# A new instruction order for a gated mix of windowed attention and a token-mixing MLP, with the last result tile cut at three quarters of its columns

## The chip, the core and the metric

The kernel runs on one core of a Trainium2 chip. The metric is the device time of one execution in microseconds (us). A core has five engines that run side by side, each with its own queue of instructions: TensorE (PE; its weight loads are listed as PEld), VectorE (DVE), ScalarE (ACT), GpSimd (POOL) and SyncE (SP), which here only starts DMA transfers. Instructions of one engine stay in order; engines wait for each other through semaphores.

## What is computed

```python
def reference(A_x, A_wqkv, A_wo, B_x, B_w1, B_b1, B_w2, B_b2, gate_w):
    # x: 1 x 2048 x 512, bf16
    def _A_ref(x, wqkv, wo):                      # 32 heads of 16, causal window of 256 keys
        qkv = (x @ wqkv) ...                      # q, k, v
        scores = einsum("bhqd,bhkd->bhqk", q, k) * 16 ** -0.5
        mask = (0 <= i - j < 256)
        p = softmax(where(mask, scores, -1e9))
        return einsum("bhqk,bhkd->bhqd", p, v) ... @ wo
    def _B_ref(x, w1, b1, w2, b2):
        h = layernorm(x, axis=-1)
        u = gelu(einsum("bsd,sf->bdf", h, w1) + b1)     # S = 2048 -> F = 1376
        y = einsum("bdf,fs->bds", u, w2) + b2           # back to 2048
        return y.transpose(0, 2, 1)
    g = sigmoid((x * gate_w).sum(-1, keepdims=True))
    return g * _A_ref(x, ...) + (1 - g) * _B_ref(x, ...)
```

## The kernel before

The 2048 tokens are 16 tiles of 128. The work is cut into about 1,100 tasks, and each task issues a few instructions on one engine. The names of tasks are used all through this document:

- `x`, `xt`, `wqk`, `wv`, `gw`, `w1_`, `w2_`, `wo`: loads, on SP. `xt1` to `xt3` are transposing DMAs of 512 tokens each (L464); `gw` copies the 512 weights of the gate to all 128 partitions (L510). `vs` and `vz` copy rows of V between partitions (L720 to L731).
- `warm` fills PE before data is there (L593). `xta` transposes the first 512 tokens on PE (L610), and `xtc` copies the result out of PSUM.
- `q`, `k`, `v` are projections (L672). `q2_1.0` is the first pair of matmuls of row block 2 of q for the tokens 512 to 1023. `qc`, `kc`, `vc` copy them out of PSUM. The projections of the first 512 tokens start with two half-width matmuls, since the token columns arrive in halves.
- `s5.v1`, `s5.C`: score matmuls of query tile 5 (L923 for the full key tiles, L1024 for the corners of the window, L979 for the last tile). `e` are their exponentials on ACT (L875), `m` the masks, on POOL (L539) or DVE (L888, L955). `pv5.2`: the products with V (L1069). `n1` to `n4` normalise a tile on DVE and put it back transposed (L1160 to L1195).
- `bs`, `ba`, `pow`, `h`: layer norm on DVE and POOL. `gl`, `gatem`, `gatee`, `ez`: the gate's dot products (L803), exponentials and their spreading.
- `u`: the first MLP product (L672, and L1240 for the last 96 columns), `ub` its bias (L439, L441), `gelu` one block of four ACT instructions (L1272).
- `y`: the second MLP product of a result tile, 11 matmuls with `w2` and four with `wo` into the same PSUM bank; `f` scales it (ACT L439, DVE L442), `o` writes it to memory (L1324).

A task such as `u`, `y` or a later `q`, `k`, `v` is flexible. It runs as 128-column weights, or as four 32-column pieces side by side when its neighbours have that shape already, because a change of the shape costs PE time. The set `THEN` says after which attention task the pieces are used.

The order on each engine is not found by a scheduler at build time. `PLAN` writes it out, one string of task names for each engine, and the digits after a name are its buffers: `s1.v0:26` means that the scores go to the pairs of PSUM banks that start at 2 and at 6, `e1.v0.0:1` that the exponential goes to buffer 1. PSUM has eight banks (0 to 7). A task that takes a bank waits until the engine that used it last is done with it:

```python
if who not in (None, t.engine):
    tc.add_manual_dep(first, ins.name, ..., reason="psum bank")
```

`arrange` walks the five strings and merges them into one emission order, with cost numbers that stand in the tasks (`2.3`, `0.58` and so on). These numbers change no instruction. They decide how the engines' instructions are interleaved in the program, and for a POOL task whether it is given a wait for the DVE instruction before it[...].

Of the kernel before, what the change touches and what calls it, by code (L numbers as in the profile page):

```python
# [84 lines left out]
def arrange(tasks):  # L85
# [21 lines left out]
    while len(order) < len(tasks):  # L107
# [83 lines left out]
        warm:3 xta0.0.1:7 xta0.0.0:4 warmb xta0.1.1:5 xta0.1.0:6 q3_0.0:4 q2_0.0:1 q0_0.0:7 q3_0.1 q0_0.1 q1_0.0:3  # L191
        k3_0.0:5 k0_0.0:6 q1_0.1 k1_0.0:2 k1_0.1 q1_0.2 q0_0.2 q1_0.3 k3_0.1 k0_0.1 q0_0.3 q0_0.4 k1_0.2 k0_0.2
        k0_0.3 q1_0.4 k1_0.3 k2_0.0:0 k0_0.4 q2_0.1 k3_0.2 k1_0.4 q2_0.2 k2_0.1 k3_0.3 k3_0.4 q2_0.3 s0.v0:62
        q3_0.2 q2_0.4 k2_0.2 k2_0.3 v0.0:5 q3_0.3 k2_0.4 v0.2 s1.v0:62 q3_0.4 v2.0:0 v2.2 v3.0:5 v3.2 q0_1.0:4
        s0.v1:60 q0_1.2 q3_1.0:2 q3_1.2 v5.0:3 v5.2 s0.C:06 k2_1.0:4 k3_1.0:5 k2_1.2 s-1.C:60 k3_1.2 q1_1.0:3
        q1_1.2 s1.v2:60 v1.0:2 v1.2 v10.0:5 pv-1.0:6 v13.0:3 k3_2.0:4 v10.2 v13.2 s1.C:60 v15.0:2 v15.2 biast:5
        k2_2.0:3 k3_2.2 k2_2.2 v12.0:2 v12.2 s1.v1:04 pv0.0:6 v14.0:3 pv0.1 pv0.2 v14.2 k1_1.0:2 s1.v3:40 k1_1.2
        v7.0:3 v7.2 s2.v2:60 v6.0:2 v6.2 v4.0:4 k0_1.0:5 k0_1.2 s2.v3:26 v4.2 pv1.0:0 pv1.1 pv1.2 pv1.3 pv1.4
        v8.0:5 v8.2 s2.v0:62 q2_1.0:4 k1_2.0:5 k1_2.2 v9.0:7 v9.2 q2_1.2 s3.v1:20 k0_2.0:6 v11.0:7 k0_2.2 v11.2
        u2.0:5 s2.v1:02 u2.2 u3.0:4 u2.4 s2.C:62 u3.2 u3.4 u3.6 u3.8 s3.v0:06 u3.10 u3.12 u3.14 u2.6 s3.v3:62  # L200
        pv2.0:0 u2.8 pv2.1 pv2.2 pv2.3 u7.0:4 s3.v2:26 u7.2 u2.10 u7.4 s3.C:20 u7.6 u7.8 u7.10 s4.C:26 u2.12 u7.12
        u2.14 u7.14 s5.v0:02 pv3.0:6 pv3.1 pv3.2 q0_2.0:5 pv3.3 q0_2.2 s4.v2:20 u10.0:4 u10.2 u10.4 u10.6 s4.v0:26
        u10.8 u10.10 u10.12 u6.0:5 s4.v1:20 u10.14 u6.2 u6.4 s4.v3:06 u6.6 q3_2.0:3 u6.8 q3_2.2 u6.10 s5.v2:60
        u0.0:4 u0.2 u0.4 s5.v3:62 u0.6 pv4.0:0 pv4.1 u6.12 u0.8 pv4.2 pv4.3 s5.v1:26 u6.14 u0.10 u0.12 s5.C:02
        u0.14 q2_2.0:5 q2_2.2 s6.v3:06 k3_3.0:4 k3_3.2 q1_2.0:3 q1_2.2 u5.0:2 s6.v1:46 u5.2 u5.4 u1.0:3 u1.2
        s6.v2:04 pv5.0:6 pv5.1 u1.4 u1.6 pv5.2 pv5.3 u5.6 s6.v0:04 u1.8 u1.10 u1.12 s6.C:46 u5.8 u5.10 u1.14
        s8.v1:04 u5.12 u5.14 pv6.0:6 pv6.1 pv6.2 pv6.3 s7.v2:40 k1_3.0:2 k1_3.2 u4.0:3 s7.v0:06 u4.2 u4.4 u9.0:2
        s7.C:04 u4.6 u4.8 u4.10 s8.v0:64 u4.12 u9.2 u4.14 u9.4 s7.v1:04 u9.6 q0_3.0:3 q0_3.2 s8.C:60 u9.8 u9.10
        u9.12 s7.v3:64 u8.0:3 u9.14 u8.2 u8.4 s10.v0:06 u8.6 u8.8 u8.10 u8.12 pv7.0:4 s8.v2:60 pv7.1 u8.14 pv7.2
        pv7.3 q2_3.0:2 s8.v3:60 k0_3.0:3 k0_3.2 q3_3.0:5 q3_3.2 q2_3.2 pv8.0:0 pv8.1 pv8.2 pv8.3 k2_3.0:6 q1_3.0:3  # L210
        k2_3.2 q1_3.2 y0.0:2 y7.0:7 s9.v2:04 y4.0:6 y0.2 y0.4 y0.6 y0.8 y7.2 y0.10 y0.11 y0.13 y4.2 y4.4 y4.6
        s9.v3:20 y4.8 y4.10 y4.11 y4.13 s9.C:24 y7.4 y7.6 y2.0:6 s10.v3:04 y7.8 y2.2 y2.4 y7.10 s11.v2:24 y7.11
        y2.6 y7.13 y2.8 s9.v0:40 y2.10 y2.11 y8.0:7 y8.2 s9.v1:42 y2.13 y8.4 y8.6 s10.v1:04 y8.8 y1.0:6 y8.10 y8.11
        s10.v2:02 y8.13 pv9.0:4 pv9.1 y1.2 pv9.2 pv9.3 s10.C:02 y9.0:7 y9.2 y9.4 s12.v2:40 y9.6 y1.4 y9.8 y1.6
        s12.C:24 y9.10 y1.8 y9.11 y1.10 y9.13 s11.v0:02 y1.11 pv10.0:4 y1.13 pv10.1 pv10.2 pv10.3 s11.v1:20 y5.0:7
        y5.2 y10.0:6 s11.C:24 y10.2 y10.4 y10.6 s11.v3:04 y5.4 y5.6 y5.8 y5.10 s12.v0:02 y5.11 y5.13 y10.8 y10.10
        s12.v3:42 y10.11 pv11.0:0 y10.13 pv11.1 pv11.2 pv11.3 s12.v1:24 y3.0:7 y3.2 y3.4 s13.v0:40 y11.0:6 y3.6
        y3.8 y3.10 s13.v1:24 y3.11 y3.13 y11.2 s13.C:20 y11.4 y11.6 y11.8 y11.10 s13.v3:40 y11.11 y11.13 pv12.0:2
        pv12.1 pv12.2 pv12.3 s14.v1:40 y6.0:6 y6.2 y12.0:7 s13.v2:20 y6.4 y6.6 y6.8 y6.10 s14.v0:24 y12.2 y6.11
        y6.13 s14.C:02 y12.4 y12.6 pv13.0:4 pv13.1 pv13.2 pv13.3 s14.v2:02 y12.8 y12.10 y13.0:6 y12.11 s15.C:04  # L220
        y12.13 y13.2 s14.v3:20 y13.4 y14.0:7 y13.6 y13.8 y13.10 s15.A:40 pv14.0:2 pv14.1 pv14.2 pv14.3 y14.2 y13.11
        s15.B:04 y14.4 y15r.0:3 y14.6 y14.8 y15l.0:2 y15r.2 y14.10 pv15.0:0 pv15.1 pv15.2 y15r.4 y15r.6 y15r.8
        y14.11 y15l.2 y13.13 y15l.4 y15r.10 y14.13 y15l.6 y15l.8 y15r.11 y15r.13 y15l.10 y15l.11 y15l.13
    """,
    ACT="""
        xtc0.0.0 xtc0.0.1 kc0_0 kc1_0 kc3_0 e0.v0.1:a e0.v0.0:6 kc2_0 vc0 e1.v0.0:8 vc2 e1.v0.1:b e0.v1.0:9
        e0.v1.1:7 vc3 e0.C.0:4 e0.C.1:5 vc5 e-1.C.1:3 e-1.C.0:2 kc3_1 gatee0 e1.v2.0:0 kc2_1 vc1 e1.v2.1:2 vc10
        vc13 e1.C.1:3 vc15 e1.C.0:1 kc3_2 kc2_2 vc12 e1.v1.0:a e1.v1.1:9 vc14 e1.v3.1:6 kc1_1 e1.v3.0:7 e2.v2.0:c
        vc7 e2.v2.1:d kc0_1 e2.v3.1:8 e2.v3.0:6 vc8 e2.v0.0:b e2.v0.1:a kc1_2 vc9 e3.v1.1:e e3.v1.0:f kc0_2
        e2.v1.1:9 e2.v1.0:7 e2.C.0:3 e2.C.1:2 e3.v0.1:4 e3.v0.0:5 ub3 e3.v3.1:b e3.v3.0:a e3.v2.0:c e3.v2.1:d  # L230
        e3.C.0:9 e3.C.1:8 e4.C.0:3 e4.C.1:2 ub7 e5.v0.1:4 e5.v0.0:5 e4.v2.0:9 e4.v2.1:e e4.v0.0:f e4.v0.1:d
        e4.v1.1:c e4.v1.0:8 e4.v3.0:7 e4.v3.1:6 e5.v2.0:1 e5.v2.1:0 e5.v3.1:f e5.v3.0:d e5.v1.0:e e5.v1.1:c
        e5.C.0:8 e5.C.1:9 e6.v3.1:7 gatee1 e6.v3.0:6 gatee2 e6.v1.0:h e6.v1.1:g e6.v2.0:4 e6.v2.1:5 gatee3
        e6.v0.1:f e6.v0.0:e e6.C.0:d e6.C.1:c e8.v1.1:1 e8.v1.0:0 ub1 e7.v2.1:h e7.v2.0:g e7.v0.0:7 e7.v0.1:6
        e7.C.1:a e7.C.0:b e8.v0.1:d e8.v0.0:c e7.v1.0:f e7.v1.1:e e8.C.0:3 e8.C.1:2 e7.v3.0:5 e7.v3.1:4 e10.v0.1:9
        e10.v0.0:8 e8.v2.0:7 e8.v2.1:e e8.v3.1:f e8.v3.0:6 gelu e9.v2.0:i e9.v2.1:e e9.v3.0:j e9.v3.1:c e9.C.1:g
        e9.C.0:2 e10.v3.1:f e10.v3.0:3 e11.v2.1:b e11.v2.0:a e9.v0.0:d e9.v0.1:h e9.v1.0:7 e9.v1.1:6 e10.v1.0:0
        e10.v1.1:1 e10.v2.0:5 e10.v2.1:d e10.C.0:h e10.C.1:g e12.v2.0:j e12.v2.1:i e12.C.0:4 e12.C.1:e e11.v0.0:c
        e11.v0.1:2 f1:2 e11.v1.0:d e11.v1.1:f e11.C.1:9 e11.C.0:5 e11.v3.0:h e11.v3.1:g e12.v0.1:8 e12.v0.0:3
        e12.v3.0:7 e12.v3.1:c f10:0 e12.v1.1:f e12.v1.0:d e13.v0.0:9 e13.v0.1:6 e13.v1.0:a e13.v1.1:b e13.C.1:2  # L240
        e13.C.0:g e13.v3.1:h e13.v3.0:5 e14.v1.1:e e14.v1.0:4 e13.v2.0:i e13.v2.1:j e14.v0.0:f e14.v0.1:c e14.C.0:8
        e14.C.1:d e14.v2.0:9 e14.v2.1:5 e15.C.0:3 e15.C.1:7 e14.v3.1:2 e14.v3.0:i e15.A.0:j e15.A.1:0 e15.B.0:i
        e15.B.1:h f13:1 f14:2 f15r:3
    """,
    DVE="""
        zeros parity const bs3:0 bs1:1 xtc0.1.0 xtc0.1.1 ba1 bs0:1 ba3 ba0 bs2:0 ba2 qc0_0 qc1_0 bs6:0 bs5:1 qc2_0
        h0 qc3_0 gl0 gl1 h1 gl3 qc0_1 h2 gl2 gl5 h3 gatem0 qc3_1 ba5 qc1_1 bs7:1 ba6 ba7 n1-1:c bs8:1 ez0 bs4:0
        biasc ba4 ba8 bs9:0 n2-1 bs11:1 nz-1:1 ba9 n3-1:0 m1.C.1 n10:4 bs13:0 n20 ba11 ba13 bs10:1 bs12:0 ba10 vc6
        ba12 bs15:1 bs14:0 ba15 nz0:1 ba14 h9 h11 vc4 n11:0 h12 h10 h15 h5 h14 h8 h7 h6 h13 h4 qc2_1 vc11 m2.v0.1
        m2.v2.0 n30:1 gl7 m2.C.0 m2.v1.0 m2.v1.1 n21 m2.C.1 gl8 gl6 gl13 gl12 m3.v1.1 n12:6 m3.v0.1 gl4 gl11 nz1:1  # L250
# [39 lines left out]
def kernel(  # L290
# [205 lines left out]
    def small_loads():  # L496
# [8 lines left out]
            ),  # L505
            nc.sync.dma_start(biases[N1:NB, :], B_b2[:].rearrange("(t p) -> t p", p=P)),
        ]

    dgw = load(
        "gw", lambda: nc.sync.dma_start(gwr[:], bass.AP(tensor=gate_w.tensor, offset=gate_w.offset, ap=[[0, P], [1, D]])),  # L510
        1.2, 2.3,
    )

    def set_constants():
        nc.vector.memset(eps[:], EPS)
# [876 lines left out]
```

## Time and profile before

The median of 7 runs was 201.0 us (200.54 to 201.48). The profile is of one execution.

| | before |
|---|---|
| profiled execution | 200.54 us |
| its span, first to last instruction | 198.8 us |
| around the span | 1.74 us |
| PE busy | 188.1 us (95%), 4140 matmuls recorded |
| ACT busy | 171.3 us (86%) |
| DVE busy | 153.5 us (77%) |
| POOL busy | 83.6 us (42%) |
| granted TensorE clock | 1.000 |

Consecutive instructions of one engine overlap a little, so busy times are sums of durations and not of occupied time. For PE, the distance between the starts of neighbouring matmuls is the better measure, and the text uses it. Some 33 of the 4173 matmuls have no record in the trace; each leaves what looks like a gap of one matmul.

### The profile page before, as it was taken

How to read it: one execution, taken by the hardware profiler on the slowest of the kernel's cores; microseconds unless marked ns; L12 is line 12 of the kernel's file. 1: busy time of each engine (PE TensorE's matmuls, PEld its weight loads, DVE VectorE, ACT ScalarE, POOL GpSimd, SP SyncE). 2: the span in 40 equal slices, each digit the busy share in tenths (PEclk: the TensorE clock that was granted, in tenths of full speed). 3: DMA queues.
4: the chain of work that ended last, by engine and by line, in shares of the span. 5: the costliest groups of instructions: out<-in, count | busy, mean ns of one | idle time of the engine just before them, and what ended most of it. 6: DMA issues, size and time to landing. Idle time of an engine off the chain costs nothing.

```text
span 198.8 us, 9301 instructions
## 1 busy us (share of the span) xinstructions
PE 188.1 (95%) x4140; PEld 93.7 (47%) x4173; DVE 153.5 (77%) x323; ACT 171.3 (86%) x200; POOL 83.6 (42%) x122
## 2 busy tenths in 40 slices
PE   6999989999998999999999999999999999999993
PEld 3643344434445635454544554433636354545572
DVE  2889977998898997897879689538388847595871
ACT  2299989999989887979999799799899999898743
POOL 8911499933024551651170940055553100566410
PEclk9999999999999999999999999999999999999999
DMA  5999789993010100101299740003111011112002
GB/s 146 357 174 210 188 252 278 360 319 80 3 32 3 35 0 13 22 5 32 40 389 407 290 157 2 31 30 91 50 33 56 3 57 31 44 32 62 30 3 79
DMA packets 23187, 22.02 MB, mean 111 GB/s; under 512 B 7564, under 2 KB 21260, under 8 KB 23148
## 3 DMA queue, kind: packets, MB, share of 16 engines
q1 hardware_dynamic: 23148, 21.44, 36.5%
q8 instruction: 32, 0.52, 1.2%
q14 instruction: 7, 0.06, 0.1%
HBM read 15.60 MB, written 2.10 MB: 89 GB/s over the span
## 4 chain that ended last, share of the span: by engine, by line
PE 81%; POOL 7%; ACT 6%; issue 3%; DVE 2%; POOLq 0%; DVEq 0%; ACTq 0%
PE pb L672 58%; PE ps L1069 9%; PE ps L923 9%; POOL et L539 4%; ACT et L875 4%; PE ps L1024 3%; PE pb L1240 2%; POOL VA L577 1%; ACT XT L875 1%; POOL XT L539 1%; ACT XT L604 1%; ACT KT L604 1%; PE pb L610 1%; ACT VA L604 0%; DVE ug L441 0%
## 5 line engine op out<-in xcount | busy, mean ns | idle before, releaser
L875 ACT ACTIVATE et<-ps 128x1024 bf16<-128x1024 f32 (+1 forms) x92 | 86.0, 991 | 5.0 <-PE ps L923 1.7
L539 POOL TENSOR_SCALAR_AFFINE_SELECT et<-et 128x512 bf16<-128x512 bf16 (+3 forms) x61 | 46.6, 774 | 64.3 <-ACT et L875 20.6
L875 ACT ACTIVATE XT<-ps 128x1024 bf16<-128x1024 f32 x62 | 60.7, 1027 | 8.0 <-PE ps L923 4.7
L672 PEld LDWEIGHTS <-wb 128*32 128x32 bf16 (+3 forms) x644 | 30.5, 97 | 33.6 <-issue 5.7
L672 PE MATMUL pb<-ug,wb 128*32 128x512 bf16 (+6 forms) x367 | 43.2, 369 | 1.2 <-issue 1.1
L539 POOL TENSOR_SCALAR_AFFINE_SELECT XT<-XT 128x512 bf16<-128x512 bf16 (+1 forms) x34 | 24.3, 722 | 39.9 <-ACT XT L875 14.7
L672 PE MATMUL pb<-h,wb 128*32 128x512 bf16 (+1 forms) x256 | 37.9, 380 | 1.9 <-issue 1.7
L672 PE MATMUL pb<-XT,wqkv 128*128 128x512 bf16 (+2 forms) x197 | 31.5, 371 | 1.0 <-issue 0.5
L1160 DVE STREAM_TRANSPOSE et<-ps 128x1024 f32<-128x1024 f32 (+1 forms) x16 | 19.5, 1216 | 12.1 <-PE ps L1069 11.8
L1069 PEld LDWEIGHTS <-VA 128*32 128x32 bf16 (+1 forms) x1056 | 20.2, 97 | 7.9 <-issue 3.0
L923 PE MATMUL ps<-QZ,KT 32*128 32x256 bf16 (+1 forms) x496 | 23.1, 265 | 0.1
L756 DVE TENSOR_TENSOR QZ<-pb,par 128x1024 bf16<-128x1024 f32 x16 | 19.3, 1215 | 2.1 <-PE pb L672 2.0
L672 PEld LDWEIGHTS <-wqkv 128*128 128x128 bf16 (+1 forms) x202 | 12.1, 97 | 13.0 <-issue 1.7
L1069 PE MATMUL ps<-et,VA 128*32 128x128 bf16 (+2 forms) x600 | 18.1, 216 | 0.0
L672 PE MATMUL pb<-wo,xo 128*32 128x512 bf16 (+2 forms) x155 | 17.6, 375 | 0.3 <-issue 0.2
L923 PEld LDWEIGHTS <-KT 32*128 32x128 bf16 x496 | 7.4, 92 | 22.0 <-ACT et L875 8.4
L442 DVE TENSOR_SCALAR ot<-pb,c,c 128x512 bf16<-128x512 f32 (+1 forms) x9 | 7.0, 781 | 13.2 <-PE pb L672 13.2
L672 PE MATMUL pb<-wqkv,XT 128*128 128x512 bf16 (+1 forms) x84 | 16.0, 380 | 0.6 <-issue 0.3
L1069 PE MATMUL ps<-XT,VA 128*32 128x128 bf16 (+1 forms) x456 | 14.3, 217 | 0.3 <-POOL XT L539 0.3
L1069 PEld LDWEIGHTS <-VZ 128*32 128x32 bf16 x832 | 13.2, 98 | 0.9 <-issue 0.5
L1069 PE MATMUL ps<-et,VZ 128*32 128x64 bf16 x576 | 12.8, 193 | 0.3 <-issue 0.3
L772 DVE BATCH_NORM_STATS2 stats<-xo 128x6 f32<-128x512 bf16 x16 | 10.5, 677 | 2.7 <-DMA xo<-in_A_x_dram 2.7
(78 smaller groups left out, 203.3 us busy)
## 6 DMA issues: line engine op xcount, KB each, us to landing
wb<-in_B_w_dram SPq DMA_DIRECT2D x8, 512.0 KB, 8.1
wb<-in_B_w_dram SPq DMA_DIRECT2D x2, 2048.0 KB, 10.0
VZ<-VA SPq DMA_DIRECT2D x26, 70.0 KB, 2.5
xo<-in_A_x_dram SPq DMA_DIRECT2D x3, 512.0 KB, 4.5
out_dram<-ot SPq DMA_DIRECT2D x12, 128.0 KB, 1.7
wb<-in_B_w_dram SPq DMA_DIRECT2D x4, 352.0 KB, 5.3
wqkv<-in_A_wqkv_dram SPq DMA_DIRECT2D x4, 256.0 KB, 4.8
wb<-in_B_w_dram SPq DMA_DIRECT2D x1, 1024.0 KB, 8.6
```

Source lines behind the costliest of these rows:

```text
L442: return nc.vector.tensor_scalar(out=out_, in0=in_, scalar1=scale, scalar2=bias, op0=ALU.mult, op1=ALU.add)
L539: return nc.gpsimd.affine_select(out=out_, in_=in_, pattern=[[0, n] for n in pattern] + [[step, HB]], compare_op=op, fill=0.0, base=base_, ...
L604: return nc.scalar.activation(out_(), in_(), ACT.Copy)
L672: made.append(nc.tensor.matmul(buf(b)[c:z_, c0:c0 + w_], lhsT=lhsT[:, c:z_], rhs=rhs, start=(j == 0), stop=(j == n - 1), skip_group_check= ...
L756: lambda k=k, b=b: nc.vector.tensor_tensor(out=QZ[:, k, :, (i % NQ) * SB:(i % NQ + 1) * SB], in0=buf(b)[:, None, :].to_broadcast([P, 2, SB ...
L772: f"bs{t_}", {"DVE": 0.67}, lambda b=b, t_=t_: nc.vector.bn_stats(buf(b)[:], xo[:, t_, :]),
L875: lambda e=e, b=b, shape=shape: nc.scalar.activation(out=shape(buf(e)), in_=shape(buf(b)), func=ACT.Exp, scale=SCALE),
L923: made.append(nc.tensor.matmul(to[:, :, done:done + m], lhsT=keys(j if x == "A" else j - 1, k)[rows], rhs=q[rows], start=True, stop=True, ...
L1024: made.append(nc.tensor.matmul(buf(b2[r // 2])[m_:m_ + HB, at:at + P], lhsT=keys(t_, k)[rows, a:a + HB], rhs=q[rows], start=True, stop=Tru ...
L1069: return lambda: nc.tensor.matmul(to(), lhsT=v() if callable(v) else v, rhs=buf(e)[rows, col:col + n], start=first, stop=last, tile_positi ...
L1160: lambda: nc.vector.transpose(out=view(buf(tr).bitcast(FP32)), in_=view(buf(o))), [last], takes=[tr], uses=[o],
L1240: nc.tensor.matmul(buf(bl)[to:to + 32, c0:c0 + w], lhsT=w1[gl][:, t_, wl + 32 * n:wl + 32 * n + 32], rhs=h[:, t_, a:a + w], start=(t_ == 0 ...
```

## The change

The five strings of `PLAN` and the set `THEN` are replaced. Every task stays, and PE and SP keep their tasks. Nine tasks move from DVE to ACT (`xtc0.1.0`, `xtc0.1.1`, `vc4`, `vc6`, `vc11`, `ub9`, `f6`, `f8`, `f15l`) and six from ACT to DVE (`kc1_1`, `kc1_2`, `vc5`, `vc9`, `f10`, `f15r`); 29 masks go from DVE to POOL and 29 from POOL to DVE. The cost number of `gw` goes from 1.2 to 2.5, and the last result tile is cut into 384 and 128 columns instead of 256 and 256 (`W3` is 384).

```diff
 PLAN = dict(
     PE="""
-        warm:3 xta0.0.1:7 xta0.0.0:4 warmb xta0.1.1:5 xta0.1.0:6 q3_0.0:4 q2_0.0:1 q0_0.0:7 q3_0.1 q0_0.1 q1_0.0:3
-        k3_0.0:5 k0_0.0:6 q1_0.1 k1_0.0:2 k1_0.1 q1_0.2 q0_0.2 q1_0.3 k3_0.1 k0_0.1 q0_0.3 q0_0.4 k1_0.2 k0_0.2
-        k0_0.3 q1_0.4 k1_0.3 k2_0.0:0 k0_0.4 q2_0.1 k3_0.2 k1_0.4 q2_0.2 k2_0.1 k3_0.3 k3_0.4 q2_0.3 s0.v0:62
-        q3_0.2 q2_0.4 k2_0.2 k2_0.3 v0.0:5 q3_0.3 k2_0.4 v0.2 s1.v0:62 q3_0.4 v2.0:0 v2.2 v3.0:5 v3.2 q0_1.0:4
-        s0.v1:60 q0_1.2 q3_1.0:2 q3_1.2 v5.0:3 v5.2 s0.C:06 k2_1.0:4 k3_1.0:5 k2_1.2 s-1.C:60 k3_1.2 q1_1.0:3
-        q1_1.2 s1.v2:60 v1.0:2 v1.2 v10.0:5 pv-1.0:6 v13.0:3 k3_2.0:4 v10.2 v13.2 s1.C:60 v15.0:2 v15.2 biast:5
...
-        s15.B:04 y14.4 y15r.0:3 y14.6 y14.8 y15l.0:2 y15r.2 y14.10 pv15.0:0 pv15.1 pv15.2 y15r.4 y15r.6 y15r.8
-        y14.11 y15l.2 y13.13 y15l.4 y15r.10 y14.13 y15l.6 y15l.8 y15r.11 y15r.13 y15l.10 y15l.11 y15l.13
+        warm:6 xta0.0.1:4 xta0.0.0:7 warmb xta0.1.0:5 xta0.1.1:6 q3_0.0:0 q2_0.0:5 q1_0.0:3 q2_0.1 q0_0.0:7
+        k1_0.0:2 k3_0.0:6 q0_0.1 q1_0.1 q3_0.1 q2_0.2 k2_0.0:1 k0_0.0:4 q0_0.2 q0_0.3 q1_0.2 q0_0.4 q2_0.3 k1_0.1
+        q1_0.3 q1_0.4 k0_0.1 q2_0.4 q3_0.2 k1_0.2 k3_0.1 k1_0.3 k3_0.2 k1_0.4 k2_0.1 k3_0.3 k3_0.4 k0_0.2 k0_0.3
+        k0_0.4 k2_0.2 q3_0.3 k2_0.3 q3_0.4 k2_0.4 s1.v0:26 v0.0:5 v3.0:4 v3.2 s-1.C:02 v0.2 v5.0:7 s0.v0:20 v5.2
+        v2.0:4 q0_1.0:6 q0_1.2 v2.2 s0.C:20 k3_1.0:7 k3_1.2 q3_1.0:5 q3_1.2 s1.v3:02 q1_1.0:6 q1_1.2 k2_1.0:7
+        s1.v2:24 k2_1.2 v1.0:1 v1.2 pv-1.0:2 v10.0:0 v10.2 v13.0:6 s0.v1:42 v13.2 k3_2.0:7 k2_2.0:0 k3_2.2 k2_2.2
...
+        y13.6 y13.8 y14.0:6 y14.2 s15.A:40 pv14.0:2 pv14.1 pv14.2 pv14.3 y14.4 y14.6 s15.B:04 y13.10 y14.8 y15l.0:2
+        y14.10 y15l.2 y13.11 pv15.0:4 pv15.1 pv15.2 y15r.0:3 y13.13 y14.11 y15l.4 y15r.2 y15r.4 y15l.6 y15r.6
+        y14.13 y15r.8 y15l.8 y15r.10 y15l.10 y15r.11 y15r.13 y15l.11 y15l.13
     """,
     ACT="""
-        xtc0.0.0 xtc0.0.1 kc0_0 kc1_0 kc3_0 e0.v0.1:a e0.v0.0:6 kc2_0 vc0 e1.v0.0:8 vc2 e1.v0.1:b e0.v1.0:9
...
-        e15.B.1:h f13:1 f14:2 f15r:3
+        xtc0.0.0 xtc0.1.0 xtc0.1.1 xtc0.0.1 kc1_0 kc3_0 kc0_0 kc2_0 e1.v0.0:1 e1.v0.1:6 e-1.C.1:7 e-1.C.0:2 vc3
+        e0.v0.0:4 e0.v0.1:a vc0 vc2 e0.C.0:5 e0.C.1:b gatee0 kc3_1 e1.v3.1:3 e1.v3.0:0 e1.v2.0:9 e1.v2.1:8 vc1
...
+        e15.A.1:f e15.B.1:h e15.B.0:g f13:1 f14:2 f15l:0
     """,
     DVE="""
-        zeros parity const bs3:0 bs1:1 xtc0.1.0 xtc0.1.1 ba1 bs0:1 ba3 ba0 bs2:0 ba2 qc0_0 qc1_0 bs6:0 bs5:1 qc2_0
...
+        zeros bs3:0 parity ba3 bs1:1 bs0:0 ba1 bs2:1 ba2 const ba0 qc0_0 qc1_0 qc2_0 gl0 qc3_0 h2 gl5 gl1 gl3 gl2
+        bs5:0 vc5 ba5 gatem0 qc0_1 bs7:1 bs4:0 qc3_1 ba7 ba4 bs6:1 qc1_1 ba6 n1-1:c ez0 n2-1 bs8:0 h7 nz-1:1 bs9:1
...
     POOL="""
-        ident ones masks blanks pow0 m1.v0.1 m-1.C.1 m-1.C.0 m1.v0.0 m0.v0.0 m0.C.1 m0.v0.1 m0.v1.0 m0.v1.1 m0.C.0
...
+        ident masks blanks ones pow0 m-1.C.1 m0.v0.1 m0.v0.0 m-1.C.0 m1.v0.0 m1.v3.1 m1.v0.1 m1.v3.0 m0.C.1 pow1
...
     SP="""
-        x0.0 x0.2 wqk0 wqk1 wqk2 wqk3 x1.4 wv xt1 gw xt2 w1_20 x2.8 vs0 xt3 bias x3.12 w1_03 vs1 vs2 w1_01 w1_10
-        w1_22 w1_00 w1_21 w1_02 w1_23 w1_11 w1_13 w1_12 vz7:2 vz2:0 vz3:1 vz4:0 vz6:1 vz5:0 vz12:0 vz8:1 wo w2_0
-        w2_1 w2_2 o0 o4 o7 vz9:2 vz10:1 o2 o8 vz11:2 o9 o1 o5 o10 o3 o11 vs13 vz13:0 o6 vz14:2 o12 o13 o14 o15r
-        o15l
+        x0.0 x0.2 wqk0 wqk1 wqk2 wqk3 gw wv x1.4 xt1 x3.12 xt2 x2.8 vs0 xt3 w1_21 bias w1_23 vs1 w1_03 w1_20 w1_13
+        w1_12 vs2 w1_00 w1_01 w1_02 w1_11 w1_10 vz2:1 vz8:0 w1_22 vz3:2 vz4:1 vz5:2 wo vz9:1 vz6:2 w2_0 vz7:2 w2_1
+        w2_2 vz10:2 vs13 vz11:0 o4 o0 o2 o7 o8 o9 o1 o5 o10 vz13:0 vz12:2 vz14:1 o3 o11 o6 o12 o13 o14 o15r o15l
     """,
 )
...
     dgw = load(
         "gw", lambda: nc.sync.dma_start(gwr[:], bass.AP(tensor=gate_w.tensor, offset=gate_w.offset, ap=[[0, P], [1, D]])),
-        1.2, 2.3,
+        2.5, 2.3,
     )
...
-        parts = [("", 0, D)] if t_ < NT - 1 else [("l", 0, D // 2), ("r", D // 2, D)]
+        parts = [("", 0, D)] if t_ < NT - 1 else [("l", 0, W3), ("r", W3, D)]
```

In the SP string `gw` stands seventh, ahead of `wv` and `x1.4`; before it stood tenth, behind `xt1`.

## The prediction

> **What bounds the kernel now.** I read the page first: engines, slices and the chain that ended last.
>
> ```profile
> span 198.8 us, 9301 instructions
> PE 188.1 (95%) x4140; PEld 93.7 (47%) x4173; DVE 153.5 (77%) x323; ACT 171.3 (86%) x200; POOL 83.6 (42%) x122
> PE   6999989999998999999999999999999999999993
> PE 81%; POOL 7%; ACT 6%; issue 3%; DVE 2%; POOLq 0%; DVEq 0%; ACTq 0%
> ```
>
> PE is full in almost every slice and carries 81% of the chain, so an order can win only what PE loses between its matmuls. To see how much that is, I compared PE's queue with the starts of its matmuls in the timeline. Three rates fit: a 128x512 matmul takes 0.216 us from start to start and a 256 wide one 0.109; four 32-column pieces of 512 together take as long as one 512; a change of the weights' shape costs 0.118 us beyond that (median of the changes to and from L923). Summed in queue order from `q3_0.0`, which starts at 6.12, they place `pv-1.0` at 24.71; the trace has it at 24.66. So the rates hold, and what the trace shows beyond the sum is waiting.
>
> The whole stream of before sums to 187.15 us: 163.6 of matmul columns at 2.4 a nanosecond, 175 changes of shape of 0.118 = 20.7, and 2.9 of small change (about 2 ns a matmul). It took 189.43 (6.12 to 195.55, where the last matmul is issued). **PE waits 2.28 us in all.** That is the most a perfect order could take back. Three places hold two thirds:
>
> ```profile
> 24.66 0.20 PE L1069 MATMUL ps<-et,VA 64*32 64x64 bf16 x1
> 25.23 0.19 PE L1069 MATMUL ps<-et,VS 64*32 64x64 bf16 x1 [0.37 <-POOL et L539]
> 25.71 0.38 PE L672 MATMUL pb<-wqkv,XT 128*128 128x512 bf16 x1 [0.16 <-issue]
> ```
>
> `pv-1.0` starts and stands until POOL has masked the second half of its exponentials: 0.5 us are not made up. At 63.34 `pv3.2` waits 0.48 for a mask on POOL, and `pv8.2` at 117.7 loses 0.49, without a releaser in the record. The remaining 0.8 are pieces of 0.1 or less. Gaps of 0.22 elsewhere vanish again one matmul later; they are missing records.
>
> Then the two ends, from the timeline (SP and the tail):
>
> ```profile
> 3.75 0.43 SPq L455 DMA_DIRECT2D xo<-in_A_x_dram  x1
> 4.23 0.51 SPq L476 DMA_DIRECT2D wqkv<-in_A_wqkv_dram  x1
> 4.78 6.10 SPq L464 DMA_TRANSPOSE XT<-in_A_x_dram  x1
> 10.93 0.57 SPq L510 DMA_DIRECT2D gwr<-in_gate_w_dram  x1
> 11.55 4.33 SPq L464 DMA_TRANSPOSE XT<-in_A_x_dram  x1
> ```
>
> ```profile
> 195.20 0.57 ACT L439 ACTIVATE junk<-pb,c,c 128x256 bf16<-128x256 f32 x1
> 195.75 0.55 DVE L442 TENSOR_SCALAR ot<-pb,c,c 128x256 bf16<-128x256 f32 x1 [1.68 <-PE pb L672]
> 195.79 0.33 SPq L1324 DMA_DIRECT2D out_dram<-junk  x1
> 196.32 0.33 SPq L1324 DMA_DIRECT2D out_dram<-ot  x1
> ```
>
> In the first the reader sees the order of the early loads, in the second that after PE's end only `f15l` on DVE (0.55) and its store remain: 3.25 us to the end of the span.
>
> **The change, part by part.** *PE's own work.* The columns are the same; some 2,560 of them change from the whole to the four-piece form, at the same rate. The changes of shape are 174 instead of 175. The new stream sums to 187.03: **-0.12**.
>
> *The quarter.* 15 matmuls of 128 columns and 15 of 384 stand for 30 of 256. The nearest row is L610 at 5.23 (8 matmuls with 128-column weights in 0.61 us, that is 56 ns from start to start), against 53 for the columns alone, so the cut costs nothing. [...]
>
> *The tail.* `y15l` still ends last, but its `f15l` now has 384 columns and runs on ACT: between 0.57 (256) and 0.78 (512), so 0.67 instead of 0.55. `y15r` ends 4 x 0.16 = 0.64 ahead of it, its `f15r` of 128 columns on DVE (an estimate of 0.4 from 0.55 and 0.81 for 256 and 512) is through before, and its store of 0.33 on SP is issued before `o15l` is ready. The last store carries 96 KB instead of 64; stores of 64 KB land in 1.5, of 128 in 1.7. **+0.15** (0.1 to 0.3).
>
> *The gate's weights.* The words say late, but in SP's queue `gw` moves forward, past `wv`, `x1.4` and `xt1`. The windows show what it does to the DMA queues:
>
> ```profile
> core 0: us, PE busy (x) PEld busy (x) DVE busy (x) ACT busy (x) POOL busy (x), PEclk, DMA share, GB/s
> 7.50:10.00 2.50, 2.50 (x14) 1.25 (x13) 2.06 (x5) 0.00 (x0) 2.29 (x4) 1.00 1.05 354
> 12.50:15.50 3.00, 3.00 (x22) 1.19 (x20) 2.07 (x3) 3.00 (x5) 0.00 (x0) 1.00 1.05 81
> ```
>
> In the 3 us in which its 128 packets run, the queues move 81 GB/s instead of 354, so they lose 3.0 x (1 - 81/354) = 2.3 us. [...] everything behind `gw` is late by 0.8 (its packets alone, 8 per engine at about 0.1) to 2.3. The packets of `xt1` ended at 12.5; now 13.3 to 14.8. Its first user was `q0_1.0` at 16.5 and becomes `v5.0` at 15.6. `wv` and `x1.4`, 1.5 us of packets each behind a `gw` that starts near 7.5, end by 11.3 and 12.8 at the latest; `v0.0` wants the one at 13.5, `gl5` on DVE the other at 14.6. No wait, but 1 us of cover is left where there were 4. `xt3` stands behind `vs0`, which now waits for `vc0` until 19.6 instead of 17; it lands near 25.1 and `v13.0` wants it at 25.9.
>
> *The start.* All eight q and k chains of the first tokens now run before the first scores, so `s1.v0` is at 13.15 where `s0.v0` was at 11.62, and ACT starts later. I walked ACT's queue with the trace's spacings (an exponential 0.91, a copy 0.48; a result is there 0.42 after its last matmul's start, the end of an instruction 0.11 after its slot).
> - `q0_0.4` wants `wqk3` at 8.29; PEld waited for it until 8.32: 0.1.
> - `kc2_0` 13.24, `e1.v0` 13.72 and 14.64, ending 15.66; `v5.0` takes bank 7 from it at 15.56: 0.14.
> - `e-1.C` 15.54 and 16.04, ending 16.63. `s0.v0` takes both pairs, at 16.25: 0.43. Behind it stand `v5.2`, `v2` and `q0_1`; `kc`, `vc` and DVE's `qc0_1` follow late by the same.
> - `pv-1.0` comes at 24.9. Its masks, now near the head of POOL's queue, are done by 22 and `vs0` lands by 22.5: the 0.5 of before is gone.
> - `s2.v3` at 34.8 wants the bank of `n10`, which ends at 34.85: 0.1.
>
> About **0.8** up to 46 us, where before has 0.85. ACT also takes on 2.0 us of work (+2 `xtc` of 0.55, +1 `vc` 0.6, +1 `ub` 0.7, +1 `f` 0.78, -2 `kc` of 0.6) which DVE loses. In the windows ACT's durations sum to 8.3 to 9.9 of each 10 us and overlap by about 0.11 each, so 1 us or more of ten is free, and that covers it; without it PE would pay up to 2.0.
>
> *The rest.* Before loses 1.4 here. `pv8.2` comes 7 us after its last score task where it was 3.3 after it, and `m3.v2` moves from POOL to DVE, so both 0.5 should go. The 29 masks that go each way between POOL (0.66 each) and DVE (0.43) leave both sums as they were. The gelu block can start near 116.1 in place of 117.7, while its first user `y4.0` comes at 118.3; `w2_0` waits for `u1` (92.9) where it left SP at 98.06 before; `w1_22`, now behind `vz8` and so behind `vc9` (near 47), is wanted at 62. I keep 0.4 for small pieces. No view shows a new wait, which proves little over 450 tasks: 0.2 to 2.0.
>
> **Sum.** PE 187.03 + 0.8 + 0.4 = 188.2 against 189.43: -1.2. Tail +0.15. Net -1.05, so 200.54 becomes 199.5 in an execution like the profiled one. That one is the fastest of the seven, 0.46 under the median of 201.0; the median becomes **199.9**.
>
> **Rivals.** *The waits only move* (20 in 100). Each order leaves PE some 2.3 us[...]. For it: the unexplained 0.49, and the 0.8 that come back at the start. Then -0.12 + 0.15: 201.0.
>
> *The gate's weights starve the first V tiles* (10 in 100, slower). `v5.0` stands in PE's queue ahead of everything else, and if `xt1` lands after 15.7, PE waits for the difference. The gain of 1.05 is used up at 16.8. The end of 14.8 above plus 2 us more for the transposes behind it (packets of them took up to 2.2 us in the trace) gives 16.8 to 17.3; at 17.3 the time is 201.5. Against it: 1 us of cover by the upper estimate.
>
> *More goes than I count* (15 in 100): nothing after 46 us and less at the start, PE 187.03 + 0.5, with the tail -1.75: 199.2.
>
> *My forecast* has 55 in 100, and by itself 199.4 to 200.4 (waits 0.7 to 1.7).
>
> A time within 0.2%, 200.6 to 201.4, is about what cannot be told from no change. The forecast gives almost all of its 55 to faster, the third rival its 15, the first 5 of its 20 (an error of a few tenths); same gets 14 and slower 11. The range goes from 199.0 to 201.3.
>
> **What would show it.** Right: `pv-1.0` without a pause near 25; gaps near 15.6 and 16.3 that end with ACT; PE's last matmul near 194.3; ACT L439 128x384 of about 0.67 at the end. Wrong: PE waiting for a DMA of XT near 15.7; POOL or ACT releasing PE for 0.5 or more after 46 us[...].

## The result, and the profile after

The changed kernel takes 200.6 us (median of 24 runs, 199.98 to 201.24). The kernel before, run on the same chip, takes 201.29. The ratio is 0.9965, with a 95% interval of 0.9954 to 0.9976: a third of a per cent faster. The forecast was 199.9. The profiled execution took 199.98 us, 0.56 less than the one of before, and its span is 0.5 us shorter.

The head of the page, with the same rows as before, and the engines' shares of the chain that ended last:

```profile
span 198.3 us, 9306 instructions
PE 187.1 (94%) x4147; PEld 93.5 (47%) x4182; DVE 151.3 (76%) x320; ACT 172.4 (87%) x203; POOL 80.3 (41%) x122
PE   6998999899999999999999999999999999999993
PE 87%; ACT 6%; issue 3%; DMA 1%; DVE 1%; DVEq 0%; ACTq 0%
```

PE is as full as it was. POOL has left the chain, where it had 7%. The method of the prediction gives the rest: the starts of PE's matmuls, less the sum of PE's own work at the rates of the trace. PE's work from `q3_0.0` on is 187.03 us, as worked out, and the sum of its waits is **1.57 us where before has 2.28**. The gain of 0.71 and the 0.12 of work are paid back in part: `q3_0.0` starts at 6.19 instead of 6.12, and the tail is 0.25 longer. 0.71 + 0.12 - 0.07 - 0.25 = 0.51, which is the difference of the spans within a few hundredths.

The waits have not become fewer everywhere. Up to 46 us PE loses 0.98 where before loses 0.85; behind that 0.59 where before loses 1.43. Two places that lost 0.97 together are gone there. One is `pv8.2`, to which the last experiments come back. The other is `pv3.2`, for which before has a mask on POOL as the releaser (timelines of before and of after, PE):

```profile
63.34 0.41 PE L1069 MATMUL ps<-XT,VA 128*32 128x128 bf16 x16 [0.31 <-POOL XT L539]
```

```profile
62.79 0.40 PE L1069 MATMUL ps<-et,VA 128*32 128x128 bf16 x16
```

The order of before pauses there with the same releaser in all three of its traces. In after the masks of `s3.v2` are on DVE. No run moves them alone, so that this is the cause is read from the traces and not tried.

Of the pieces on PE that hold most of the waiting up to 46 us, three end with ACT or DVE, and the one that was dear before is gone (timeline, PE and its weight loads):

```profile
15.81 0.12 PEld L672 LDWEIGHTS <-XT 128*32 128x32 bf16 x8 [0.49 <-ACT et L875]
...
16.80 0.40 PE L923 MATMUL ps<-QZ,KT 32*128 32x256 bf16 x8 [0.37 <-ACT et L875]
...
24.94 0.20 PE L1069 MATMUL ps<-et,VA 64*32 64x64 bf16 x1
...
35.23 0.40 PE L923 MATMUL ps<-QZ,KT 32*128 32x256 bf16 x8 [0.27 <-DVE et L1160]
```

The rows are `v5.0`, `s0.v0`, `pv-1.0` and `s2.v3`. By the sum they lose 0.18, 0.42, nothing and 0.29. `pv-1.0` runs through without a releaser.

The early loads (SP), the two stretches of the prediction's windows, and the tail:

```profile
3.75 0.43 SPq L510 DMA_DIRECT2D gwr<-in_gate_w_dram  x1
4.22 0.43 SPq L476 DMA_DIRECT2D wqkv<-in_A_wqkv_dram  x1
4.70 0.65 SPq L455 DMA_DIRECT2D xo<-in_A_x_dram  x1
5.40 6.86 SPq L464 DMA_TRANSPOSE XT<-in_A_x_dram  x1
```

```profile
core 0: us, PE busy (x) PEld busy (x) DVE busy (x) ACT busy (x) POOL busy (x), PEclk, DMA share, GB/s
7.50:10.00 2.50, 2.50 (x15) 1.37 (x14) 1.49 (x7) 0.00 (x0) 2.34 (x4) 1.00 0.99 230
12.50:15.50 3.00, 3.00 (x42) 1.08 (x40) 2.81 (x7) 2.52 (x4) 0.00 (x0) 1.00 1.13 262
```

```profile
194.34 0.41 DVE L442 TENSOR_SCALAR junk<-pb,c,c 128x128 bf16<-128x128 f32 x1 [1.02 <-PE pb L672]
194.78 0.33 SPq L1324 DMA_DIRECT2D out_dram<-junk  x1
194.99 0.67 ACT L439 ACTIVATE ot<-pb,c,c 128x384 bf16<-128x384 f32 x1 [0.76 <-PE pb L672]
195.69 0.33 SPq L1324 DMA_DIRECT2D out_dram<-ot  x1
```

The gate's weights have moved to the front of SP's queue, and with them the slow stretch of the DMA queues: 230 GB/s between 7.5 and 10 us instead of 354, and 262 instead of 81 between 12.5 and 15.5. In the tail the narrow result (128 columns) is through DVE and stored before the wide one (384 columns) leaves ACT.

### The profile page after: what moved, and what is told of

Read it like the earlier page. It is cut to its first block, busy times and chain, and to the rows that moved or that the text cites. A ratio compares the mean times of both kernels' runs of the same rounds, so it can differ in the third digit from the quotient of the medians.

```text
span 198.3 us, 9306 instructions
## 1 busy us (share of the span) xinstructions
PE 187.1 (94%) x4147; PEld 93.5 (47%) x4182; DVE 151.3 (76%) x320; ACT 172.4 (87%) x203; POOL 80.3 (41%) x122
## 4 chain that ended last, share of the span: by engine, by line
PE 87%; ACT 6%; issue 3%; DMA 1%; DVE 1%; DVEq 0%; ACTq 0%
PE pb L672 62%; PE ps L1069 10%; PE ps L923 10%; ACT et L875 4%; PE ps L1024 3%; DMA xo<-in_A_x_dram 1%; PE pb L1240 1%; ACT VA L604 1%; PE pb L610 1%; DVE et L1160 1%; ACT KT L604 1%; ACT XT L875 1%; ACT ot L439 0%; PE ps L979 0%; ACT XT L604 0%
## 5 line engine op out<-in xcount | busy, mean ns | idle before, releaser
L539 POOL TENSOR_SCALAR_AFFINE_SELECT et<-et 128x512 bf16<-128x512 bf16 (+2 forms) x66 | 46.3, 714 | 75.0 <-ACT et L875 27.2
L875 ACT ACTIVATE XT<-ps 128x1024 bf16<-128x1024 f32 (+1 forms) x58 | 55.3, 999 | 6.7 <-PE ps L923 4.2
L672 PE MATMUL pb<-ug,wb 128*32 128x512 bf16 (+5 forms) x348 | 41.9, 372 | 1.5 <-issue 1.4
L539 POOL TENSOR_SCALAR_AFFINE_SELECT XT<-XT 128x512 bf16<-128x512 bf16 (+3 forms) x29 | 21.4, 743 | 32.1 <-ACT XT L875 22.5
L1160 DVE STREAM_TRANSPOSE et<-ps 128x1024 f32<-128x1024 f32 x13 | 16.2, 1250 | 12.5 <-PE ps L1069 12.4
L1069 PE MATMUL ps<-et,VA 128*32 128x128 bf16 (+1 forms) x640 | 18.3, 219 | 0.0
L672 PE MATMUL pb<-wo,xo 128*32 128x512 bf16 (+3 forms) x175 | 17.8, 375 | 0.1
L1069 PE MATMUL ps<-XT,VA 128*32 128x128 bf16 (+2 forms) x416 | 13.8, 214 | 0.0
L442 DVE TENSOR_SCALAR ot<-pb,c,c 128x512 bf16<-128x512 f32 x8 | 6.4, 805 | 9.4 <-PE pb L672 9.4
L1195 DVE STREAM_TRANSPOSE xo<-zt 128x512 bf16<-128x512 bf16 (+1 forms) x17 | 11.4, 673 | 0.2
```

What stands on the lines that cost most here:

```text
L442: return nc.vector.tensor_scalar(out=out_, in0=in_, scalar1=scale, scalar2=bias, op0=ALU.mult, op1=ALU.add)
L539: return nc.gpsimd.affine_select(out=out_, in_=in_, pattern=[[0, n] for n in pattern] + [[step, HB]], compare_op=op, fill=0.0, base=base_, ...
L672: made.append(nc.tensor.matmul(buf(b)[c:z_, c0:c0 + w_], lhsT=lhsT[:, c:z_], rhs=rhs, start=(j == 0), stop=(j == n - 1), skip_group_check= ...
L875: lambda e=e, b=b, shape=shape: nc.scalar.activation(out=shape(buf(e)), in_=shape(buf(b)), func=ACT.Exp, scale=SCALE),
L1069: return lambda: nc.tensor.matmul(to(), lhsT=v() if callable(v) else v, rhs=buf(e)[rows, col:col + n], start=first, stop=last, tile_positi ...
L1160: lambda: nc.vector.transpose(out=view(buf(tr).bitcast(FP32)), in_=view(buf(o))), [last], takes=[tr], uses=[o],
```

## The experiments

Every ratio is to the kernel before, with its 95% interval; after itself is 0.9965. "Waits" is PE's sum of waits in the profiled execution by the method above. Edits are made to after unless stated otherwise.

**The gate's weights back behind `xt1`.**

```diff
-wqk3 gw wv x1.4 xt1 x3.12
+wqk3 wv x1.4 xt1 gw x3.12
```

> The kernel after with the gate's weights behind xt1 in SP's queue, where they stood before. Theory: the new DVE order asks for them at 12.3 (gl0 stands ahead of qc3_0), so DVE stands until they land near 15; qc3_0 then ends near 17, s-1.C waits for its bank, and PE ends 1.2 to 2 us later than in the kernel after. Rival: DVE has slack here and the place of the load is worth nothing; PE ends within 0.2 us of the kernel after, or earlier because xt1 lands 1 us sooner.

Measured: 205.24 us, 1.0203 [1.0156, 1.0251], 4.6 us over after and far more than was expected. DVE stands for the weights, and PE stands for DVE (timeline):

```profile
16.78 0.69 DVE L803 SCALAR_TENSOR_TENSOR junk<-xo,gwr 128x512 bf16<-128x512 bf16 x1 [4.14 <-DMA gwr<-in_gate_w_dram]
...
18.76 0.32 PE L1024 MATMUL ps<-QZ,KT 32*64 32x128 bf16 x16 [3.46 <-DVE QZ L756]
```

The new DVE string has `gl0`, the first dot product of the gate, ahead of `qc3_0`, which the scores `s-1.C` need. So in this order the load in front is a condition and not a choice. The wait itself is 3.5 us. Another 1.6 comes behind it, in the windows of this kernel:

```profile
core 0: us, PE busy (x) PEld busy (x) DVE busy (x) ACT busy (x) POOL busy (x), PEclk, DMA share, GB/s
16.00:18.70 2.70, 0.00 (x0) 0.00 (x0) 1.92 (x4) 0.04 (x1) 0.00 (x0) 1.00 1.10 211
18.70:21.00 2.30, 1.91 (x40) 0.79 (x42) 2.23 (x7) 1.61 (x4) 0.00 (x0) 0.84 1.03 258
21.00:24.00 3.00, 2.76 (x8) 1.04 (x8) 2.28 (x8) 2.40 (x3) 1.98 (x4) 0.55 0.15 50
```

PEclk is the granted clock. PE does nothing for 3.5 us, and the clock falls 1.5 us after it has started again at 18.76 (the trace records it at one half from 20.27 to 23.68 us): `v2.0`, `q0_1.0`, `q0_1.2` and `v2.2` lose 0.60 + 0.42 + 0.42 + 0.13 = 1.57 with no one to wait for. A third piece, 1.07 at `pv8.2` (124 us), is of the kind of the last experiments. Up to `s0.v0` this kernel has lost 3.33 more than after; with 1.57 and 1.07 that is 5.97, and its span is 6.0 us longer (204.3). By the medians it is 4.6: this execution is 0.8 slower than the median of its kernel, and the profiled one of after 0.6 faster than its own.

**The last tile in halves again.**

```diff
-[("l", 0, W3), ("r", W3, D)]
+[("l", 0, D // 2), ("r", D // 2, D)]
```

> The kernel after with the last tile cut at 256 columns again, in the same order. Theory: the cut at 384 costs 0.15 to 0.25 us at the end, because f15l reads 384 columns instead of 256 (0.67 against 0.57 on ACT) and its store is longer, while PE's time is the same; so the end comes 0.1 to 0.25 us earlier than in the kernel after. Rival one: the quarter was worth something (r is out of the way sooner), and halves are 0.1 to 0.3 us slower. [...]

Measured: 0.9963 [0.9946, 0.9980], no difference to after. The tail, from the end of PE's issue to the end of the span, is 0.18 shorter (`f15l` has 256 columns and takes 0.56). PE loses 0.31 more just ahead of `pv15.1` at 190 us, and the two cancel within what can be told. The cut into quarters is worth nothing that these runs can tell.

**The quarter alone, on the kernel before.** The same cut with before's order (`D // 2` to `W3`).

> The kernel before with only the cut of the last tile at 384 columns. Theory: f15l on DVE goes from 0.55 to about 0.68 and the store grows, 0.15 to 0.25 us at the end. In this order only y15r.0, y15l.0 and y15r.2 stand ahead of pv15, so the cut takes 0.1 us of filling away there instead of adding some. Ratio 1.001 to 1.0015. Rival: the cut is what makes the kernel after faster; then the ratio is 0.998 or below.

Measured: 1.0006 [0.9988, 1.0023]. It brings nothing by itself that can be told; with the run above, what after gained comes from the order.

**Masks, on the kernel before.** The masks of `s-1.C` first in POOL's queue, and one mask of `pv8` moved from POOL to DVE.

```diff
-pow0 m1.v0.1 m-1.C.1 m-1.C.0 m1.v0.0
+pow0 m-1.C.1 m-1.C.0 m1.v0.1 m1.v0.0
-m8.v3.1 m8.v3.0 m9.C.0
+m8.v3.1 m9.C.0
-kc0_3 qc3_3 qc2_3
+kc0_3 m8.v3.0 qc3_3 qc2_3
```

> The kernel before with two edits: on POOL the masks of m-1.C stand ahead of m1.v0.1, and m8.v3.0 moves from POOL to DVE, ahead of qc3_3. Theory: the 0.5 us that PE waits at pv-1.0 near 25 go and stay gone, ratio 0.9975; at pv8.2 (117.7) the mask is ready 0.26 us sooner, so if POOL is the cause there PE's loss goes from 0.49 to 0.23. Rival for the first: it comes back at pv0 or at a score task before 46 us. Rival for the second: the loss at pv8.2 stays at 0.49, since it was code fetch and not the mask.

Measured: 1.0003 [0.9983, 1.0022]. The edit failed in its first half. With the corner's masks at the head, POOL stood 12.8 us for the exponentials of `s-1.C` and began to mask at 23.52; `pv-1.0` paused as before. The cause lies further up: in before, `s-1.C` itself starts only at 21.27, in after at 14.95. The second half is no evidence either: `m8.v3.0` is wanted by `pv8.3` and not by `pv8.2`, and `pv8.2` lost 0.26 here, but 0.23 in the run above, where its masks are untouched. Nor was the 0.5 that `pv8.2` lost in the first profile the mask's: PE stood on weights from VZ, which `pv8.1` uses and `pv8.2` does not (the row is shown below), so it had not come to `pv8.2` yet.

**The two new waits, one at a time.** `v5.2`, which waits for nothing, goes ahead of `s0.v0`:

```diff
-v5.0:7 s0.v0:20 v5.2
+v5.0:7 v5.2 s0.v0:20
```

> The kernel after with one swap in PE's queue: v5.2 ahead of s0.v0. Theory: PE loses 0.43 us at s0.v0 because the pairs of banks it takes are held by the exponentials of s-1.C until 16.7; v5.2 (0.43 us of matmuls) has nothing to wait for, so it fills the hole and the profile's PE end moves up by 0.4 us, the ratio to the kernel after by 0.2%. Rival: the waits only move; ACT's queue is the real limit there, and the 0.43 come back at the next score task that needs a bank (s0.C, s1.v3 or s1.v2), so PE's end stays within 0.1 us.

Measured: 0.9949 [0.9931, 0.9966]. The 0.42 at `s0.v0` is gone, but 0.17 comes back at `v2.0`, whose bank waits for ACT's copy, and 0.09 at `s0.C`. And `v7.2` ahead of `s2.v3`:

```diff
-s2.v3:24 v7.2 k0_1.0:0
+v7.2 s2.v3:24 k0_1.0:0
```

> The kernel after with v7.2 ahead of s2.v3 alone. Theory: 0.2 us of the 0.3 that PE waits there for DVE's transpose of tile 0 are won: ratio 0.9955 to before. Rival: the swap delays the exponentials of s2.v3 on ACT by what PE wins and the later stages pay; then 0.9965 or above.

Measured: 0.9950 [0.9925, 0.9976]. The 0.29 at `s2.v3` is gone, 0.11 comes back at `k0_1.0`. Either swap puts 0.2 us of work under a wait.

**Both swaps together.**

> The kernel after with v5.2 ahead of s0.v0 and v7.2 ahead of s2.v3, the last tile still cut at 384. Theory: both waits go, 0.17 us of the first as the run of that swap alone showed and 0.2 of the second's 0.3 (0.1 came back at k0_1.0 in the run with three edits); the cut at 384 keeps PE supplied ahead of pv15, so the tail loses nothing: 0.35 to 0.4 us under the kernel after, ratio 0.9945 to before. Rival: the three-edit kernel was slow because of the swap at s2.v3, not of the halves; then this one is at 0.998 or above.

Measured: 1.0002 [0.9984, 1.0020]; and with the halves as well:

> The kernel after with v5.2 ahead of s0.v0, v7.2 ahead of s2.v3 and the last tile cut in halves. Theory: the three places are independent, so 0.43 + 0.33 + 0.15 = 0.9 us come off the kernel after (0.45%), and about 1.6 us off the kernel before. Rival: waits return elsewhere, and no more than half of it (0.4 us) shows in the time.

1.0000 [0.9981, 1.0019]. Two gains of 0.15%, each no larger than the noise, make a loss of 0.37%, which is clear of it. Both traces show the two gains where they belong, 0.69 lost up to 46 us in place of after's 0.98. The loss is 50 to 140 us later, in places that the swaps do not touch. With both swaps PE loses 0.14 at `u4.4` (97.7), 0.17 at `y9.2` (144.8), 0.20 at `y12.2` (173.5), 0.52 at `s14.v1` (182.1) and 0.20 at `pv15.1` (191.3), together 1.23 us. No semaphore ends any of these, so PE waits for no other engine there. What the swaps do change there is PE's own stream: `v5.2` and `v7.2` now stand behind a task in `THEN` and run as 8 pieces instead of 2 whole matmuls. That is 12 instructions more for each, so that everything behind them stands later in the stream: 8,364 matmuls and weight loads in after, 8,376 with one swap, 8,388 with both. Two theories: the place in the stream, or the order of the two moves. Three kernels tell them apart by changing `THEN` alone.

*Both swaps, 12 instructions fewer behind 47 us* (`s3.v0` out of `THEN`):

> After with both swaps (s0.v0 behind v5.2, s2.v3 behind v7.2), as in the run where they came to 1.0002, but with s3.v0 taken out of THEN: u2.6, at about 47 us, then runs as 2 whole matmuls instead of 8 pieces, so that everything behind it stands 12 instructions nearer to the start of PE's queue, as in the runs with one swap. It costs one change of the weights' shape more (+0.12 us). If the loss of the two swaps together comes from where the late instructions lie in PE's stream: ratio 0.9945 to 0.9965 (200.3 to 200.7 us) and no loss near 182 us. If the two moves hinder each other between 16 and 46 us, or elsewhere by their order: 1.0 to 1.001 (201.2 to 201.5).

*Both swaps, 24 fewer behind 70 us* (`pv4.2` out):

> The same two swaps, with pv4.2 taken out of THEN: u0.14 and u6.8, at about 70 us, run as whole matmuls, and everything behind them stands 24 instructions nearer to the start, as in after itself. Two changes of shape more (+0.24 us). Position in the stream: 0.995 to 0.997. The order of the two moves: 1.0005 to 1.002.

*One swap, 12 more behind 78 us* (`pv5.1` in):

> After with only the swap of s2.v3 and v7.2 (0.995 in its run), with pv5.1 added to THEN: u1.6, at about 78 us, runs as 8 pieces instead of 2 whole matmuls, which moves everything behind it 12 instructions on, as with both swaps; the order of the tasks is that of the better run. One change of shape fewer (-0.12 us). Position in the stream: the loss comes without the second swap, 0.9985 to 1.0005 (about 201.0 us). The order of the two moves: 0.9935 to 0.9955 (200.0 to 200.4).

| kernel | order | matmuls and weight loads | ratio [95%] | waits |
|---|---|---|---|---|
| after | after's | 8,364 | 0.9965 [0.9954, 0.9976] | 1.57 |
| one swap (`s2.v3`) | one | 8,376 | 0.9950 [0.9925, 0.9976] | 1.49 |
| one swap, 12 more | one | 8,388 | 1.0011 [0.9989, 1.0033] | 2.80 |
| both swaps | both | 8,388 | 1.0002 [0.9984, 1.0020] | 2.32 |
| both, 12 fewer | both | 8,376 | 0.9960 [0.9937, 0.9983] | 1.75 |
| both, 24 fewer | both | 8,364 | 0.9950 [0.9927, 0.9973] | 0.99 |

The ratio goes with the number of instructions and not with the order: the two kernels with 8,388 are near 1.000, and the four with fewer at 0.995 to 0.9965. Each of the three fell where the place in the stream was to put it (the third 0.0006 above), and none where the order of the moves was.

**Where it pauses.** The place is sharp enough to be counted. Here are the weight loads that begin after four of the pauses (PE's weight loads in the timelines of before, of both swaps, of the one with 12 more, and of the halves); after, at the numbers of the first and of the second, runs through (the last fence):

```profile
117.00 0.10 PEld L1069 LDWEIGHTS <-VZ 128*32 128x32 bf16 x2
117.55 0.11 PEld L1069 LDWEIGHTS <-VZ 128*32 128x32 bf16 x6 [0.46 <-issue]
```

```profile
181.75 0.09 PEld L672 LDWEIGHTS <-wb 128*32 128x32 bf16 x1 [0.61 <-issue]
```

```profile
181.63 0.09 PEld L672 LDWEIGHTS <-wb 128*32 128x32 bf16 x1 [0.59 <-issue]
```

```profile
190.12 0.11 PEld L672 LDWEIGHTS <-xo 128*32 128x32 bf16 x5 [0.30 <-issue]
```

```profile
117.88 0.16 PEld L1069 LDWEIGHTS <-VZ 128*32 128x32 bf16 x8
...
181.41 0.66 PEld L672 LDWEIGHTS <-wb 128*32 128x32 bf16 x16 [0.21 <-issue]
```

"Issue" says that the engine waited for nothing that the profile shows. Each pause is inside a task, between two instructions of a group that otherwise start within 10 ns. In the order in which PE's instructions are emitted, its matmuls, weight loads and semaphore instructions counted, PE goes on with the weight load of number 4,546 in the first, 7,618 in the second and third, about 8,130 in the fourth; within one or two, these numbers leave 194 when divided by 256. The other four losses of both swaps lie at such numbers too: about 3,778, 5,570, 7,106 and 8,130. So all of these pauses stand at the ends of blocks of 256 instructions. The page lists how the code comes (after, DMA queues: packets, MB, share):

```profile
q8 instruction: 32, 0.52, 1.2%
```

0.52 MB in 32 packets is 16 KB each, and 32 blocks of 256 begin between number 450 and the end of after's stream (450, 706, to 8,386), as many as the packets. In the pauses above, and in the one of 1.07 at `pv8.2` with the gate's weights moved back (number 4,546), PE goes on 2.4 to 2.7 us after the packet of the block has started. At number 7,618 that packet starts 1.9 and 2.2 us ahead of PE in the two kernels that pause for 0.5, and 2.6 to 2.7 ahead in after, in either single swap and in both swaps with 24 fewer, which do not. So a pause is a block of code that comes late. The traces show two ways to that:

- *PE runs through the block before it too fast.* It did the block ahead of number 7,618 in 2.9 us in the two kernels that pause there, and in 3.4 to 3.6 in those that do not. Dense stretches of small instructions (pieces, products with V) do that, and 12 instructions more or fewer decide whether such a stretch lies ahead of a block's end.
- *The packet starts late.* In the fourteen traces the packet of a block mostly starts after PE has come to the end of the one before (59 of the 64 of before and after do; the other five start up to 1.1 us ahead of that): by a median of 0.8 us where the other DMA queues are less than 20% busy in between (some 290 packets), of 3.0 where they are more than 60% busy (some 110). `pv8` runs while `w2` is loaded. The block ahead of number 4,546 takes 5.7 us in after and with the gate's weights moved back alike, but the packet starts 2.9 us after the block has begun in the one and 4.2 in the other, and only the other pauses, for 1.07. No run changes the loads around a packet alone, so that they hold it up is not shown beyond this.

The plan was made with this in mind: `arrange` reckons with `BLOCK, AHEAD, FETCH, BUSY = 256, 80, 3.8, 3.0`, that is 3.8 us from one block's begin to the next one's code, and 3.0 more while loads run. The traces have 0.8 + 2.5 = 3.3 us and 3.0 + 2.5 = 5.5 (2.5 from the packet's start to PE's going on).

**Pieces where they save something.** The pieces of `s1.v2` and `s3.v3` cost 36 instructions each and save no change of shape, while pieces that stand beside products with V do save one. The last kernel has both swaps, and after's length of the stream:

```diff
-v5.0:7 s0.v0:20 v5.2
+v5.0:7 v5.2 s0.v0:20
-s2.v3:24 v7.2 k0_1.0:0
+v7.2 s2.v3:24 k0_1.0:0
 THEN
-s1.v2 s3.v3
+pv2.1 pv5.1 s7.C
```

> After with both swaps, and the same length of PE's stream as after has it (24 instructions fewer than with the swaps alone), but with the four-piece form put where it saves changes of the weights' shape: THEN loses s1.v2 and s3.v3 and gains pv2.1, pv5.1 and s7.C. PE's work by the rates of the trace: 170 changes of shape in place of 176 in the run with 24 instructions fewer, 0.71 us less than there, 0.47 less than after. From about 85 us on, every task stands at the place in the stream that it had in that run. If place in the stream and changes of shape are what counts: ratio 0.9915 to 0.994 (199.5 to 200.0 us), with 0.2 to 0.5 of the gain lost if the denser pieces near 47 and 78 us outrun the code. If a change of shape is not worth 0.118 where pieces stand beside attention: 0.995 to 0.9965.

Measured: 199.8 us, **0.9936 [0.9917, 0.9956]**, the lowest of all, though its interval overlaps those of the kernels at 0.995. By the sum PE has 186.56 us of work, 0.47 less than after (170 changes of shape instead of 174, 0.118 each), and waits 1.49; from 85 us on no code comes late.

## Why the prediction held

The direction and the sum's method held; four terms of the sum were too small, one reason was wrong and one was a part. The measured 200.6 lies in the range of 199.0 to 201.3, but just outside the 199.4 to 200.4 that the forecast gave itself, although the waits of 1.57 lie in its 0.7 to 1.7: the tail and the start cost 0.17 more, and the median of 201.0 from which it subtracts became 201.29 over 61 runs.

- *PE's own work, -0.12*: held. The 128-column matmuls of `y15r` start at 193.26, 193.32 and 193.37, 56 ns apart, as in the row of L610.
- *The tail, +0.15*: 0.25. `f15l` on ACT took 0.67, as said. The miss is the store: from its issue to the end of the span 2.61 us with 96 KB, where before has 2.48 with 64.
- *The gate's weights*: the last packets of `xt1` ended near 13.7, inside 13.3 to 14.8. `v5.0` waited for ACT and not for the load, so the rival of starvation did not come about. What the prediction did not ask is what the load in front is for: moved back, it costs 4.6 us.
- *Up to 46 us, 0.8*: 0.98. `v5.0` 0.18 for 0.14, `s0.v0` 0.42 for 0.43; the walk through ACT's queue was good to a few hundredths. `s2.v3` lost 0.29 where 0.1 was worked out; its releaser was the right one, `n10` on DVE, which ended at 35.09 instead of 34.85. `wqk3` cost nothing for 0.1, and 0.09 came at `k1_2.0`.
- *The start, 0*: 0.07. This one is not the kernel's: `q3_0.0` starts between 6.07 and 6.61 in the fourteen profiled executions.
- *The rest, 0.4*: 0.59, in pieces of 0.17 (`s5.v0`), 0.15 (`q1_3.0`), 0.11 (`s15.C`) and less.
- Together 0.10 + 0.18 + 0.07 + 0.19 = 0.54, and 1.05 - 0.54 = 0.51. The mechanism was right and the gain half as large. By the medians it is 0.69.
- *`pv-1.0`, 0.5 gone*: it is gone. The reason given, its masks' place in POOL's queue, was only a part: the masks alone could not be put earlier in before. `s-1.C` starts 6.3 us earlier in after.
- *`pv3.2`, 0.48 gone*: it is gone, and the reason fits: the mask `m3.v2` that released PE is no longer on POOL.
- *`pv8.2`, 0.5 gone*: it is gone, and the step that explained it failed. The prediction named the distance to the scores and a mask that moves to DVE. The pause of before is late code, at the end of a block. In after PE comes to the same number in its stream at 117.9, 0.9 us later, while the packet starts at 115.1 as it did. That this term came true is luck: 0.49 of the 0.71 by which the waits fell. The two other traces of before's order lose only 0.26 and 0.23 there, so half of it belongs to the one execution that was profiled.
- *"The waits only move"* was the nearest rival: 1.57 of 2.28 stayed.

## What to carry to other kernels

A sum of an engine's own work at the rates of its trace, laid against its starts, finds every wait, also those for which the profile names no one; then look whether those without a releaser stand at a fixed distance in the engine's instruction stream. Where many small instructions follow each other, code is a resource with a latency (here 3.3 us from the begin of one block of 256 to the next one's code, 5.5 while loads run): an edit early in the stream can cost more 150 us later than it gains on the spot, so two edits that gain by themselves have to be measured together. Pieces that save no change of shape are only instructions; take them out first.

## What was not expected of the hardware

- Late code: up to 1.07 us in one place, in all nine places counted at the end of a block of 256 PE instructions; in five of them PE goes on 2.4 to 2.7 us after the block's packet has started. That packet starts 0.8 us after PE has come to the end of the block before where the other DMA queues are nearly idle, 3.0 where they are busy (medians). 12 instructions moved the time by 0.6% (0.9950 to 1.0011).
- With the gate's weights moved back, the pause of PE of 3.5 us was followed by a granted clock of one half for 3.4 us (20.27 to 23.68), which cost 1.6 us beyond the pause.
- The first projections run at half rate for a while in some executions of a kernel and not in others (0.92 us lost by `q0_0.4` in the trace of the masks, none in that of after). The record of the full clock begins at 5.03 us in after and at 7.54 in the trace of the masks, where 256-wide matmuls stand 0.21 us apart before it and 0.11 behind it; so this is the clock as well. It is a part of the spread of 0.6% between runs of one kernel.
